# Attention and expert layer on one core: weight decoding in another order, the last bias steps inside the first attention steps

## The chip, the cores and the metric

The kernel runs on one core of one Trainium2 chip. The metric is the device time of one execution in microseconds (us). A core has five engines that run beside each other, each through its own list of instructions in order: TensorE (PE; its weight loads are PEld), VectorE (DVE), ScalarE (ACT), GpSimd (POOL) and SyncE (SP), which here only issues DMA transfers.

## The reference, cut to what matters

```python
B, H, S, D = 4, 8, 576, 64                      # q, k, v: [B, H, S, D]
rel = pos[:, None] - pos[None, :]
x = (log1p(abs(rel)) / log1p(maximum(pos[:, None], 1)))[..., None]
bias = maximum(x @ w1 + b1, 0) @ w2             # 32 hidden units, H outputs
scores = q @ k.T / sqrt(D) + bias.transpose(2, 0, 1)[None]
attn = exp(scores - max(scores)); attn = attn / (sum(attn) + 1e-9)
x = (attn @ v), heads side by side              # [2304, 512]
h = x @ moe_w_in                                # 512 -> 2048
g = s * maximum(h, 0) ** 2 + b
out = g @ moe_w_out                             # 2048 -> 512
```

The two weight matrices arrive as 64-bit numbers and are turned into 32-bit ones on the chip.

## The kernel before, in words

Everything is one function, `attention_moe`, in which the order of the instructions is written out by hand (line 578): each engine gets its instructions in the order in which the code calls them, and the tile library adds the waits. The program has three stages.

**Bias stage** (lines 599 to 604): 36 bias steps of 16 rows each, `STEPS`. `bias_features(st)` makes four feature tiles; `kind` (line 119) says which engine makes each: v is DVE, p is POOL, a is ACT. `bias_step(st)` (line 131) multiplies them by the second weights on PE into one PSUM tile `bps`, from which ACT makes the tile `stg` (line 147), and SP stores `stg` to memory (line 153). For steps 24 to 35 `first_head` also copies the rows of head 0 straight to the tiles `bt` and `be` that the first attention steps add. `bps` lies in the pool `ps_x` (one buffer) in each third step and otherwise in `ps_s` (two buffers). The table `plan` (line 586) says what else is issued behind which bias step: loads, the splits of q and k for pair 0, and the first two scores.

**Attention** (`step`, line 525): 16 pairs of (head, two batches), five steps each, n = 5p + u. Step n turns the probabilities of n (`probs_t`: PE `tps`, copies `pt` by ACT and DVE), computes the scores of n + 2 (PE `sps`, in `ps_s`), adds the bias and takes the maximum on DVE (`biased`, L250), exponentiates on ACT (`expo`, L261) and multiplies the probabilities of pair p - 1 with v (`av`, L366 and L369, in `ps_x`). L369 belongs to u = 4 and so marks each pair once. `split_qk` lets POOL split q (at u = 0) and k (at u = 1) of pair p + 1 into a high and a low part, two instructions each (L211, L212). `norm` (u = 3, L273) makes the reciprocal sums on DVE. `fill()` takes one piece of early weight decoding into a step: eight blocks, each ACT `Abs` (L407), POOL clamp (L409), three DVE bit operations (L411, L414, L417), the high part `wh` on DVE (L426) and the low part `wl` on POOL (L429), six fills a block, at u = 0 to 3 from pair 1 on. A fill stands near the end of its step, and the split of q or k behind it.

**Expert layer** (from line 639): expand (L476) and project (L501) by slots; it also decodes the other 24 weight blocks.

SP issues all loads and stores in one order. Tiles that are placed in memory freed by the bias stage wait for its last users.

```python
        kind = (ends.get(st) or ("vvpa", "vppa", "vpvp")[st % 3])[c]
...
        if st % 3 == 2:
            ps = ps_x.tile([128, 2, 512], F32, tag="x", name="bps")
...
        if st < STEPS - 4 or st == STEPS - 1:
            for i, t in late:
...
        if cur and u < 2:
            split_qk(p + 1, u)
```

Of the kernel before, what the change touches and what calls it, by code (L numbers as in the profile page):

```python
# [9 lines left out]
F32 = mybir.dt.float32  # L10
# [4 lines left out]
ALU = mybir.AluOpType  # L15
# [11 lines left out]
def attention_moe(ctx, tc, q, k, v, w_in, w_out, dist, par, out):  # L27
    nc = tc.nc
    NB, H, S, D = 2 * q.shape[0], q.shape[1], k.shape[3] - 64, q.shape[2] // 2
    DM, DFF = w_out.shape[1], w_out.shape[0]  # L30
    NT = out.shape[0]
# [23 lines left out]
    ps_t = ps_ctx.enter_context(tc.tile_pool(name="ps_t", bufs=2, space=PSUM))  # L55
    pss_ctx = ExitStack()
    ps_s = pss_ctx.enter_context(tc.tile_pool(name="ps_s", bufs=2, space=PSUM, side="right"))
    dctx = ExitStack()
    dp = dctx.enter_context(tc.tile_pool(name="dp", bufs=1, side="right"))
    fp = dctx.enter_context(tc.tile_pool(name="fp", bufs=16, side="right"))  # L60
# [48 lines left out]
        nc.vector.tensor_copy(sb, pt_[:, 2:4])  # L109

    feats, late = {}, []
    ends = {STEPS - 4: "vvvp", STEPS - 3: "vvva", STEPS - 2: "vpva", STEPS - 1: "vpva"}

    def feature(st, c):
        w = NU - S - 16 * st - 4 * c
        f = fp.tile([128, S // 64, 68], F32, tag="f", name="f")[:, :, 0:64]
        src = ls[:, w:w + S].rearrange("p (a b) -> p a b", b=64)
        col = slice(4 * st + c, 4 * st + c + 1)
        kind = (ends.get(st) or ("vvpa", "vppa", "vpvp")[st % 3])[c]
        if kind == "v":  # L120
            nc.vector.tensor_scalar(f, src, thr[:, col], None, op0=ALU.max)
        elif kind == "p":
            nc.gpsimd.tensor_scalar(f, src, FLT_MAX, thr[:, col], op0=ALU.min, op1=ALU.max)
        else:
            nc.scalar.activation(f, src, AF.Relu, bias=off[:, col])
        return f, kind == "a"
# [4 lines left out]
    def bias_step(st):  # L131
        f2, f0, f3, f1 = feats.pop(st)
        fs = (f0, f1, f2, f3)
        if st % 3 == 2:
            ps = ps_x.tile([128, 2, 512], F32, tag="x", name="bps")
        else:
            ps = ps_s.tile([128, 2, 512], F32, tag="s", name="bps")
        pb = ps.rearrange("p a b -> p (a b)")
        for c in range(4):
            nc.tensor.matmul(  # L140
                pb[32 * c:32 * c + 32, 0:512], w2bd, fs[c][0][:, 0:8], start=True, stop=True)
        for c in range(4):
            nc.tensor.matmul(
                pb[32 * c:32 * c + 32, 512:S], w2bd, fs[c][0][:, 8:9], start=True, stop=True)
        kcol = kc[:, 1:2] if fs[3][1] else kc[:, 0:1]
        stg = fp.tile([128, S], F32, tag="stg", name="stg", bufs=10)
        nc.scalar.activation(stg, pb[:, 0:S], AF.Identity, scale=nr[:, st:st + 1], bias=kcol)  # L147
        if st >= 24:
            first_head(st, stg)
        late.append((st, stg))  # L150
        if st < STEPS - 4 or st == STEPS - 1:
            for i, t in late:
                nc.sync.dma_start(out=bias_d[:, 16 * i:16 * i + 16, :].rearrange("h r j -> r h j"), in_=t)
            late.clear()
# [16 lines left out]


    qs, ks, vals, tts, bts, pts, units, accs = {}, {}, {}, {}, {}, {}, {}, {}
    sums, rows, rts, rbs, bes, xts = {}, {}, {}, {}, {}, {}

    def load_bias(p, t0, t1):
        h = pairs[p][0]
# [44 lines left out]
    def scores(n):  # L222
        p, t = divmod(n, 5)
        qt, kt = qs[p], ks[p]
        c = slice(128 * t, 128 * t + 128)
        xs = range(width(n))
        ps = [ps_s.tile([128, 2, 512], F32, tag="s", name="sps") for _ in xs]
        mms = []
        for hf in range(2):
            for x in xs:  # L230
                d = slice(64 * x, 64 * x + 64) if t < 4 else slice(0, 128)
                o = hf * HALF + (64 if x == 0 else 0)
                for i, (a, b) in enumerate(((0, 0), (0, 1), (1, 0))):
                    mms.append((i, hf, x, ps[x][:, hf, 0:HALF], qt[d, a, c], kt[d, b, o:o + HALF]))
        for i, _, _, o, a, b in sorted(mms, key=lambda e: e[1::-1]):
            nc.tensor.matmul(o, a, b, start=(i == 0), stop=(i == 2))  # L236
        units[n] = (
            tp.tile([128, 2, S], F32, tag="pr", name="pr"),
            sm.tile([128, 2], F32, tag="mn", name="mn"),
            ps,  # L240
        )
        if t == 0:
            sums[p] = sm.tile([128, 9], F32, tag="su", name="su")

    def biased(n, x):
        p, t = divmod(n, 5)
# [10 lines left out]
    def expo(n, x):  # L257
        p, t = divmod(n, 5)
        pr, mn, _ = units[n]
        col = 4 * x + t if t < 4 else 8  # L260
        nc.scalar.activation(  # L261
            pr[:, x], tts.pop((n, x)), AF.Exp, bias=mn[:, x:x + 1], scale=-1.0,
            accum_out=sums[p][:, col:col + 1])

    def width(n):
        return 2 if n % 5 < 4 else 1
# [2 lines left out]


    def norm(p):
        su = sums.pop(p)
        nc.vector.tensor_scalar(su, su, 1e-9, None, op0=ALU.add)  # L273
        nc.vector.reciprocal(su, su)
        rows[p] = su

# [12 lines left out]
    def probs_t(n):  # L289
        p, t = divmod(n, 5)  # L290
        if p not in pts:
            pts[p] = (ptp.tile([128, 4, 2, S], F32, tag="pt", name="pt"),
                      ptp.tile([128, S], F32, tag="ptr", name="ptr"))
        pt, ptr = pts[p]
        halves = [slice(64 * r, 64 * r + 64) for r in range(2)]

# [122 lines left out]
        w_full[kind, g, i] = full  # L419
        yield  # L420

    def split_w(kind, g, i):
        full = w_full.pop((kind, g, i))
        hi, lo = w_hi[kind, g][:, i], w_lo[kind, g][:, i]
        if g == 0:
            nc.vector.tensor_copy(hi, full)  # L426
        else:
            nc.scalar.activation(hi, full, AF.Copy)  # L428
        nc.gpsimd.tensor_tensor(lo, full, hi.bitcast(F32), op=ALU.subtract)  # L429


    chunks = [(t0, min(512, NT - t0)) for t0 in range(0, NT, 512)]
    NC = len(chunks)
# [91 lines left out]
    def step(n):  # L525
        p, u = divmod(n, 5)
        m = n + 2
        cur = 0 <= n < LAST
        if cur:
            probs_t(n)  # L530
        if cur and u == 3:
            norm(p)
        if ok(m, 0):
            scores(m)
            for x in range(width(m)):
                biased(m, x)
            expo(m, 0)
        if p >= 1:
            av(p - 1, u, 0)
            av(p - 1, u, 1)  # L540
            if u < 4:
                fill()
        if n == 0:
            load_be(1)
        if u == 4 and cur:
            norm_store(p)
        if u == 0 and p > 0:
            if n <= LAST:
                norm_load(p - 1)
            if p > 1:  # L550
                store_xt(p - 2)
            if cur:
                load_be(p + 1)
                load_v(p + 1)
                load_q(p + 2)
                load_k(p + 2)
        if cur and u < 2:
            split_qk(p + 1, u)
        if cur:
            for e in loads_at.get((p, u), ()):  # L560
                load_bias(*e)

    early = [(kind, 0, i) for kind in range(2) for i in range(4)]

    def early_work():
        for j, e in enumerate(early):
            if j + 2 < len(early):
                load_w(*early[j + 2])
            yield from decode_w(*e)
            split_w(*e)  # L570
            yield

    filler = early_work()

    def fill():
# [12 lines left out]
        11: ((load_bias, 0, 0, 1),),  # L588
        17: ((load_bias, 0, 1, 2),),
        20: ((load_v, 0), (load_be, 0)),  # L590
        28: ((split_qk, 0, 0),),
        30: ((split_qk, 0, 1),),
        26: ((load_bias, 0, 2, 3),),
        33: ((scores, 0), (biased, 0, 0), (expo, 0, 0), (biased, 0, 1)),
        35: ((expo, 0, 1), (scores, 1), (biased, 1, 0),
             (expo, 1, 0), (biased, 1, 1), (load_w, *early[0]), (load_w, *early[1]),
             (load_q, 2), (load_k, 2), (load_v, 1)),
    }
    for st in range(STEPS):
        if st + 2 < STEPS:  # L600
            bias_features(st + 2)
        bias_step(st)
        for fn, *args in plan.get(st, ()):
            fn(*args)
    dctx.close()
    ctx.enter_context(tc.tile_pool(name="pad2", bufs=1, side="right")).tile([128, 40], F32, name="pad2")
    wg0 = ctx.enter_context(tc.tile_pool(name="wg0", bufs=1, side="right", reuse_waits="tile"))
    alloc_w(0, wg0)
    wf = ctx.enter_context(tc.tile_pool(name="wf", bufs=1, side="right", reuse_waits="tile"))
    pctx = ExitStack()  # L610
    ptp = pctx.enter_context(tc.tile_pool(name="ptp", bufs=2, side="right", reuse_waits="tile"))
    decoding = {}

    def late_start(e):
# [5 lines left out]
        for _ in decoding.pop(e):  # L620
            pass

    for n in range(LAST - 2):
        step(n)
        if n == LAST - 10:
            for _ in filler:
                pass
            for a in range(KB - 1):
                load_x(0, a)
        if n == LAST - 4:  # L630
            load_x(0, KB - 1)
# [15 lines left out]
    pctx.close()  # L647
    ps_ctx.close()
    op = ctx.enter_context(tc.tile_pool(name="op", bufs=1, reuse_waits="tile"))
    acc = [op.tile([128, DM], F32, name=f"acc{k}") for k in range(NT // 128)]  # L650
    ps_o = ctx.enter_context(tc.tile_pool(name="ps_o", bufs=1, space=PSUM, reuse_waits="tile"))

    for a in range(KB):
# [104 lines left out]
```

## Time and profile before

| | us |
|---|---|
| median of 3 runs | 686.18 (686.15 to 689.35) |
| the profiled execution | 689.37 |
| its span, first to last instruction | 687.5 |
| PE busy | 665.2 (97%) |
| DVE busy | 456.4 (66%) |
| ACT busy | 353.6 (51%) |
| POOL busy | 181.5 (26%) |
| bias stage, up to the last `bps` | 55 |
| attention, up to the first L476 | 55 to 286 |
| expert layer | 286 to 687 |

The page divides the span among the engines; the trace then gives each instruction's start, its length and, in brackets, how long its engine had been idle and what released it. A share of the whole span says little here, since the three stages have different limits: the last stage is read from the windows, the first two from the timelines of single engines. The profiled execution is the longer kind of the runs: it lies 3.2 us above the median.

### The profile page before, as it was taken

How to read it: one execution, taken by the hardware profiler on the slowest of the kernel's cores; microseconds unless marked ns; L12 is line 12 of the kernel's file. 1: busy time of each engine (PE TensorE's matmuls, PEld its weight loads, DVE VectorE, ACT ScalarE, POOL GpSimd, SP SyncE). 2: the span in 40 equal slices, each digit the busy share in tenths (PEclk: the TensorE clock that was granted, in tenths of full speed). 3: DMA queues.
4: the chain of work that ended last, by engine and by line, in shares of the span. 5: the costliest groups of instructions: out<-in, count | busy, mean ns of one | idle time of the engine just before them, and what ended most of it. 6: DMA issues, size and time to landing. Idle time of an engine off the chain costs nothing.

```text
span 687.5 us, 13641 instructions
## 1 busy us (share of the span) xinstructions
PE 665.2 (97%) x5202; PEld 508.2 (74%) x5202; DVE 456.4 (66%) x883; ACT 353.6 (51%) x741; POOL 181.5 (26%) x190
## 2 busy tenths in 40 slices
PE   8987999999999999999999999999999999999997
PEld 4435667667676667578888888888888888888886
DVE  7996889988898888556576346665446655343344
ACT  6997767777677777534544333332333332322221
POOL 7992362345523450002222012121012220000000
PEclk9999999999999999999999999999999999999999
DMA  5976865656646734378745643216345204333312
GB/s 162 300 233 173 301 206 174 210 190 188 201 147 200 228 114 145 98 235 295 245 153 177 251 153 137 103 37 245 122 154 189 87 35 150 127 119 122 123 61 92
DMA packets 53872, 114.84 MB, mean 167 GB/s; under 512 B 10800, under 2 KB 18224, under 8 KB 53808
## 3 DMA queue, kind: packets, MB, share of 16 engines
q1 hardware_dynamic: 53664, 113.65, 49.8%
q8 instruction: 41, 0.67, 0.4%
q10 hardware_dynamic: 144, 0.33, 0.1%
q14 instruction: 23, 0.19, 0.1%
HBM read 83.77 MB, written 29.56 MB: 165 GB/s over the span
## 4 chain that ended last, share of the span: by engine, by line
PE 85%; DVE 4%; DMA 3%; POOL 3%; ACT 2%; issue 1%; SPq 1%; DVEq 0%; ACTq 0%; POOLq 0%
PE hps L476 29%; PE o L501 28%; PE sps L236 8%; PE xps L366 8%; PE tps L299 5%; PE bps L140 3%; PE xps L369 2%; DMA bias<-stg 2%; DVE tt L250 1%; POOL kr L212 1%; DMA qt<-in_q_dram 1%; POOL wl L429 1%; ACT stg L147 1%; POOL kr L211 1%; DMA pt__123<-in_par_dram 1%
## 5 line engine op out<-in xcount | busy, mean ns | idle before, releaser
L501 PE MATMUL o<-wh,gt 128*128 128x512 f32 x576 | 190.2, 389 | 0.0
L476 PE MATMUL hps<-x,wh 128*128 128x512 f32 (+1 forms) x640 | 181.8, 368 | 0.0
L480 ACT ACTIVATE r<-hps 128x512 f32<-128x512 f32 (+1 forms) x80 | 44.5, 556 | 212.8 <-PE hps L476 212.8
L481 DVE SCALAR_TENSOR_TENSOR r<-r,sb 128x512 f32<-128x512 f32 (+1 forms) x80 | 55.9, 698 | 143.9 <-ACT r L480 143.8
L261 ACT ACTIVATE pr<-tt,mn 128x576 f32<-128x576 f32 x144 | 110.9, 771 | 58.8 <-DVE mn L250 58.4
L476 PEld LDWEIGHTS hps<-x,wh 128*128 128x128 f32 x640 | 116.9, 188 | 22.1 <-ACT x L456 0.4
L501 PEld LDWEIGHTS o<-wh,gt 128*128 128x128 f32 x576 | 108.2, 188 | 22.3
L476 PE MATMUL hps<-x,wl 128*128 128x512 f32 (+1 forms) x320 | 117.7, 368 | 0.0
L501 PE MATMUL o<-wl,gt 128*128 128x512 f32 x288 | 112.2, 390 | 0.0
L429 POOL TENSOR_TENSOR wl<-full,wh 128x512 fp32r<-128x512 f32 x32 | 43.9, 1371 | 213.4 <-ACT wh L428 137.7
L250 DVE CUSTOM_DVE_ANT_0 tt<-sps,bt 128x576 f32<-128x576 f32 x128 | 91.3, 750 | 13.2 <-PE sps L236 12.9
L236 PE MATMUL sps<-kr,qr 64*128 64x288 f32 (+1 forms) x864 | 90.4, 310 | 7.7 <-POOL kr L212 5.1
L486 DVE SCALAR_TENSOR_TENSOR gt<-r,sb,gt 128x512 fp32r<-128x512 f32 (+1 forms) x80 | 62.7, 783 | 38.3 <-ACT gt L485 38.3
L236 PEld LDWEIGHTS sps<-kr,qr 64*128 64x128 f32 (+1 forms) x864 | 70.3, 186 | 12.3 <-POOL kr L212 6.1
L366 PE MATMUL xps<-pt,vt 128*64 128x288 f32 x512 | 77.0, 423 | 1.4 <-DVE rb L374 0.9
L485 ACT ACTIVATE gt<-r,sb 128x512 fp32r<-128x512 f32 (+1 forms) x80 | 54.4, 680 | 45.6 <-DVE r L481 45.5
L299 PEld LDWEIGHTS tps<-ident,pr 64*128 64x128 f32 x1216 | 44.7, 138 | 38.0 <-issue 27.5
L476 PEld LDWEIGHTS hps<-x,wl 128*128 128x128 f32 x320 | 60.3, 188 | 9.9
L501 PEld LDWEIGHTS o<-wl,gt 128*128 128x128 f32 x288 | 54.1, 188 | 10.5
L299 PE MATMUL tps<-ident,pr 64*128 64x64 f32 x1216 | 56.9, 230 | 4.0 <-ACT pt L330 2.0
L409 POOL TENSOR_SCALAR full<-full 128x512 f32<-128x512 f32 x32 | 23.9, 746 | 130.5 <-ACT full L407 130.1
L332 DVE COPY pt<-tps 128x512 f32<-128x512 f32 x64 | 44.0, 687 | 13.1 <-PE tps L299 13.0
(66 smaller groups left out, 704.8 us busy)
## 6 DMA issues: line engine op xcount, KB each, us to landing
x<-xs SPq DMA_DIRECT2D x48, 512.0 KB
bias<-stg SPq DMA_DIRECT2D x36, 288.0 KB
raw<-in_moe_w_in_dram SPq DMA_DIRECT2D x16, 512.0 KB
raw<-in_moe_w_out_dram SPq DMA_DIRECT2D x16, 512.0 KB
xs<-x SPq DMA_DIRECT2D x16, 512.0 KB
bt<-bias SPq DMA_DIRECT2D x7, 1152.0 KB
qt<-in_q_dram SPq DMA_DIRECT2D x16, 320.0 KB
kt<-in_k_dram SPq DMA_DIRECT2D x16, 320.0 KB
```

What stands on the lines that cost most here:

```text
L236: nc.tensor.matmul(o, a, b, start=(i == 0), stop=(i == 2))
L250: nc.vector.tensor_tensor_reduce(tt.rearrange("p (a b) -> p a b", a=2), ps[x][:, :, 0:HALF], bias.rearrange("p (a b) -> p a b", a=2), -1.0 ...
L261: nc.scalar.activation(pr[:, x], tts.pop((n, x)), AF.Exp, bias=mn[:, x:x + 1], scale=-1.0, accum_out=sums[p][:, col:col + 1])
L299: nc.tensor.matmul(outs[r], src[d], ident[d, d], is_transpose=True, start=start, stop=True, skip_group_check=not start)
L366: nc.tensor.matmul(ps[64 * x:64 * x + 64, hf, 0:HALF], vt[:, 4 * x + kb, :], pt[:, kb, x, c], start=(kb == 0), stop=False)
L429: nc.gpsimd.tensor_tensor(lo, full, hi.bitcast(F32), op=ALU.subtract)
L476: nc.tensor.matmul(ps[:, 0:n], w[0, g][:, a, fc], xs_t[s, a][:, j, 0:n], start=(i == 0), stop=(i == 3 * KB - 1))
L480: nc.scalar.activation(r, ps[:, 0:n], AF.Relu)
L481: nc.vector.scalar_tensor_tensor(r, r, sb[:, 0:1], r, op0=ALU.mult, op1=ALU.mult)
L485: nc.scalar.activation(hi, r, AF.Identity, bias=sb[:, 1:2])
L486: nc.vector.scalar_tensor_tensor(lo, r, sb[:, 1:2], hi.bitcast(F32), op0=ALU.add, op1=ALU.subtract)
L501: nc.tensor.matmul(o, gt[:, a, tok], w[1, g][:, fo], start=(fo == 0 and j == 0), stop=(fo == 3 and j == 2))
```

## The change

Four things change.

1. **The end of the bias stage.** The features of steps 32 to 35 are made as v, p, a, p, and are issued behind steps 30 to 33. Steps 30 to 35 all take `ps_x`. The first scores are issued behind step 30, the second behind step 31, attention step 0 behind step 32 and step 1 behind step 35. The stores of `stg` 30 to 35 are issued together after step 35. The q and k splits of pair 0 move from behind steps 28 and 30 to behind 23 and 25, and the loads of q and k for pair 2 and of v for pair 1 from behind step 35 to behind step 28. The buffer `pt` of even pairs gets a place of its own (`ptp0`), later used for part of the output sums.
2. **The splits of q and k** stand right behind `probs_t` in their step, ahead of that step's scores and fill.
3. **Early decoding** takes four fills a block and three fills a pair: the next block's `Abs` and clamp share fills with the present block's bit operations, and the low part `wl` is issued one fill later than `wh`, with the next block's first bit operation.
4. **`norm`** reads the sums from a tile of three rows of four, of which three are used, and writes another tile.

```diff
-    ends = {STEPS - 4: "vvvp", STEPS - 3: "vvva", STEPS - 2: "vpva", STEPS - 1: "vpva"}
...
-        kind = (ends.get(st) or ("vvpa", "vppa", "vpvp")[st % 3])[c]
+        kind = ("vpap" if st >= STEPS - 4 else ("vvpa", "vppa", "vpvp")[st % 3])[c]
...
-        if st % 3 == 2:
+        if st % 3 == 2 or st >= STEPS - 6:
             ps = ps_x.tile([128, 2, 512], F32, tag="x", name="bps")
...
-        if st < STEPS - 4 or st == STEPS - 1:
+        if st < STEPS - 6 or st == STEPS - 1:
             for i, t in late:
...
-            sums[p] = sm.tile([128, 9], F32, tag="su", name="su")
+            sums[p] = sm.tile([128, 3, 4], F32, tag="su", name="su")
...
-        su = sums.pop(p)
-        nc.vector.tensor_scalar(su, su, 1e-9, None, op0=ALU.add)
+        su = sm.tile([128, 9], F32, tag="rw", name="ru", bufs=2)
+        nc.vector.tensor_scalar(
+            su.rearrange("p (a b) -> p a b", a=3), sums.pop(p)[:, :, 0:3], 1e-9, None, op0=ALU.add)
         nc.vector.reciprocal(su, su)
...
             probs_t(n)
+            if u < 2:
+                split_qk(p + 1, u)
         if cur and u == 3:
...
-            if u < 4:
+            if u < 3:
                 fill()
...
-        if cur and u < 2:
-            split_qk(p + 1, u)
...
     def early_work():
+        ahead = {}
+
+        def begin(j):
+            if j < len(early):
+                ahead[j] = decode_w(*early[j])
+                next(ahead[j])
+
+        begin(0)
+        yield
+        next(ahead[0])
+        yield
         for j, e in enumerate(early):
             if j + 2 < len(early):
                 load_w(*early[j + 2])
-            yield from decode_w(*e)
-            split_w(*e)
+            next(ahead[j])
+            if j > 0:
+                split_lo(*early[j - 1])
             yield
+            next(ahead[j])
+            begin(j + 1)
+            yield
+            next(ahead[j])
+            if j + 1 < len(early):
+                next(ahead[j + 1])
+            yield
+            split_hi(*e)
+            yield
+        split_lo(*early[-1])
...
-        28: ((split_qk, 0, 0),),
-        30: ((split_qk, 0, 1),),
+        23: ((split_qk, 0, 0),),
+        25: ((split_qk, 0, 1),),
         26: ((load_bias, 0, 2, 3),),
-        33: ((scores, 0), (biased, 0, 0), (expo, 0, 0), (biased, 0, 1)),
-        35: ((expo, 0, 1), (scores, 1), (biased, 1, 0),
-             (expo, 1, 0), (biased, 1, 1), (load_w, *early[0]), (load_w, *early[1]),
-             (load_q, 2), (load_k, 2), (load_v, 1)),
+        28: ((load_q, 2), (load_k, 2), (load_v, 1)),
+        30: ((scores, 0), (biased, 0, 0), (biased, 0, 1), (expo, 0, 0), (bias_features, 32)),
+        31: ((expo, 0, 1), (scores, 1), (biased, 1, 0), (biased, 1, 1), (expo, 1, 0),
+             (bias_features, 33)),
+        32: ((step, 0), (bias_features, 34)),
+        33: ((bias_features, 35),),
+        35: ((step, 1), (load_w, *early[0]), (load_w, *early[1])),
     }
     for st in range(STEPS):
-        if st + 2 < STEPS:
+        if st + 2 < STEPS - 4:
             bias_features(st + 2)
         bias_step(st)
...
-    for n in range(LAST - 2):
+    for n in range(2, LAST - 2):
```

`split_lo` and `split_hi` are the two halves of the old `split_w`: the POOL subtraction and the copy of the high part.

**ACT at the end of the bias stage, from `stg` 31 before.** Before:

```order
L147 ACTIVATE stg<-bps,kc,pt__123 128x576
L125 ACTIVATE f<-ls,off 128x9x64
L147 ACTIVATE stg<-bps,kc,pt__123 128x576
L261 ACTIVATE pr,su<-tt,mn 128x576
L147 ACTIVATE stg<-bps,kc,pt__123 128x576 x2
L261 ACTIVATE pr,su<-tt,mn 128x576 x3
L330 ACTIVATE pt<-tps 128x8x64
```

Now, from `stg` 29 and 30:

```order
L147 ACTIVATE stg<-bps,kc,pt__130 128x576 x2
L261 ACTIVATE pr,su<-tt,mn 128x576
L125 ACTIVATE f<-ls,off 128x9x64
L147 ACTIVATE stg<-bps,kc,pt__130 128x576
L261 ACTIVATE pr,su<-tt,mn 128x576 x2
L125 ACTIVATE f<-ls,off 128x9x64
L147 ACTIVATE stg<-bps,kc,pt__130 128x576
L261 ACTIVATE pr,su<-tt,mn 128x576
L332 ACTIVATE pt<-tps 128x8x64
L261 ACTIVATE pr,su<-tt,mn 128x576
L125 ACTIVATE f<-ls,off 128x9x64
L147 ACTIVATE stg<-bps,kc,pt__130 128x576
```

Before, all `stg` but two were made ahead of the first exponential (L261); now five come behind it, each between exponentials, features and the copy `pt`. Behind these rows follow one feature, `stg` 34 and 35, and only then the rest of step 1.

**PE at the same place, from the first scores on.** Before:

```order
L236 MATMUL sps<-kr,qr 128x288 x12
L140 MATMUL bps<-f,pt__123 32x512 x4
L143 MATMUL bps<-f,pt__123 32x64 x4
L140 MATMUL bps<-f,pt__123 32x512 x4
L143 MATMUL bps<-f,pt__123 32x64 x4
L236 MATMUL sps<-kr,qr 128x288 x12
L299 MATMUL tps<-ident,pr 128x64 x16
L236 MATMUL sps<-kr,qr 128x288 x12
L299 MATMUL tps<-ident,pr 128x64 x16
```

Now:

```order
L236 MATMUL sps<-kr,qr 128x288 x12
L140 MATMUL bps<-f,pt__130 32x512 x4
L143 MATMUL bps<-f,pt__130 32x64 x4
L236 MATMUL sps<-kr,qr 128x288 x12
L140 MATMUL bps<-f,pt__130 32x512 x4
L143 MATMUL bps<-f,pt__130 32x64 x4
L301 MATMUL tps<-ident,pr 128x64 x16
L236 MATMUL sps<-kr,qr 128x288 x12
L140 MATMUL bps<-f,pt__130 32x512 x4
L143 MATMUL bps<-f,pt__130 32x64 x4
L140 MATMUL bps<-f,pt__130 32x512 x4
L143 MATMUL bps<-f,pt__130 32x64 x4
```

One more pair of rows (`bps` 35) and the second `tps` follow. Between the first and the second `tps` (steps 0 and 1) stand three bias steps now, and none before.

**POOL from its first instructions of the bias stage on.** Before:

```order
L123 TENSOR_SCALAR f<-ls,thr 128x9x64 x51
L211 TENSOR_SCALAR qr<-qt 128x640
L212 TENSOR_TENSOR qr<-qt,qr 128x640
L123 TENSOR_SCALAR f<-ls,thr 128x9x64 x3
L211 TENSOR_SCALAR kr<-kt 128x640
L212 TENSOR_TENSOR kr<-kt,kr 128x640
L123 TENSOR_SCALAR f<-ls,thr 128x9x64 x2
```

Now:

```order
L123 TENSOR_SCALAR f<-ls,thr 128x9x64 x43
L211 TENSOR_SCALAR qr<-qt 128x640
L212 TENSOR_TENSOR qr<-qt,qr 128x640
L123 TENSOR_SCALAR f<-ls,thr 128x9x64 x3
L211 TENSOR_SCALAR kr<-kt 128x640
L212 TENSOR_TENSOR kr<-kt,kr 128x640
L123 TENSOR_SCALAR f<-ls,thr 128x9x64 x11
```

Both splits of pair 0 stand eight features earlier, and four more features follow behind the q split of pair 1.

## Rows read from the trace of the kernel before

**Rows 1.** Windows: stretch, length, each engine's busy us, granted PE clock, DMA share, GB/s.

```profile
290.00:687.00 397.00, 393.80 (x1830) 328.26 (x1826) 210.87 (x312) 135.54 (x232) 52.48 (x48) 1.00 0.42 149
```

**Rows 2.** Timeline of PE, the u = 4 mark of pairs 0, 1, 12, 13.

```profile
83.43 1.24 PE L369 MATMUL xps<-ptr,vt 128*128 128x288 f32 x4
100.75 1.24 PE L369 MATMUL xps<-ptr,vt 128*128 128x288 f32 x4
...
256.68 1.24 PE L369 MATMUL xps<-ptr,vt 128*128 128x288 f32 x4
270.14 1.24 PE L369 MATMUL xps<-ptr,vt 128*128 128x288 f32 x4
```

**Rows 3.** Timelines of POOL and PE around step 13; in brackets idle time and releaser.

```profile
92.17 1.28 POOL L429 TENSOR_TENSOR wl<-full,wh 128x512 fp32r<-128x512 f32 x1 [2.92 <-DVE wh L426]
94.22 1.54 POOL L212 TENSOR_TENSOR kr<-kt,kr 128x640 fp32r<-128x640 f32 x1
...
95.82 1.15 PE L236 MATMUL sps<-kr,qr 64*128 64x288 f32 x10 [1.23 <-POOL kr L212]
```

**Rows 4.** Window right behind that wait, columns as in the first group.

```profile
96.00:100.00 4.00, 4.00 (x35) 2.37 (x36) 1.49 (x5) 1.63 (x4) 3.75 (x5) 0.57 1.01 355
```

**Rows 5.** Waits of PE (total us, times, longest), and its wait in pair 1.

```profile
PE sps L236 <- POOL kr L212: 5.1, 5, 1.2
...
79.99 0.92 PE L236 MATMUL sps<-kr,qr 64*128 64x288 f32 x10 [1.11 <-POOL kr L212]
```

**Rows 6.** DVE by line, 60 to 300 us: min/median/max ns, first and last start.

```profile
L414 DVE SCALAR_TENSOR_TENSOR full<-raw,full x8: 685/686/1993, 82.3 to 236.7; 128x512 uint32<-128x512 uint32 x8
L273 DVE TENSOR_SCALAR su<-su x16: 161/165/1260, 66.1 to 280.9; 128x9 f32<-128x9 f32 x16
```

**Rows 7.** Timelines of POOL and DVE in the bias stage; the q split lies between.

```profile
5.51 36.81 POOL L123 TENSOR_SCALAR f<-ls,thr 128x576 f32<-128x576 f32 x51 [4.21 <-DVE ls L100]
...
44.88 2.18 POOL L123 TENSOR_SCALAR f<-ls,thr 128x576 f32<-128x576 f32 x3
...
35.73 15.91 DVE L121 TENSOR_SCALAR f<-ls,thr 128x576 f32<-128x576 f32 x22
```

**Rows 8.** Timeline of PE: first scores, bias step 34, second `tps`.

```profile
51.35 1.05 PE L236 MATMUL sps<-kr,qr 64*128 64x288 f32 x11 [1.03 <-ACT stg L147]
53.14 1.06 PE L140 MATMUL bps<-f,pt__123 128*32 128x512 f32 x8 [0.74 <-DVE mn L250]
54.02 0.29 PE L143 MATMUL bps<-f,pt__123 128*32 128x64 f32 x8
...
59.28 0.71 PE L299 MATMUL tps<-ident,pr 64*128 64x64 f32 x16 [0.40 <-ACT pt L330]
```

**Rows 9.** Timelines of DVE and ACT: bias added, `stg`, feature, exponential, copy, first block.

```profile
52.32 0.76 DVE L250 CUSTOM_DVE_ANT_0 tt<-sps,bt 128x576 f32<-128x576 f32 x1 [0.68 <-PE sps L236]
...
49.09 0.82 ACT L147 ACTIVATE stg<-bps,kc,pt__123 128x576 f32<-128x576 f32 x1
49.81 0.77 ACT L125 ACTIVATE f<-ls,off 128x576 f32<-128x576 f32 x1
...
57.89 0.76 ACT L261 ACTIVATE pr<-tt,mn 128x576 f32<-128x576 f32 x1
...
58.65 0.57 ACT L330 ACTIVATE pt<-tps 128x512 f32<-128x512 f32 x1
...
72.99 0.65 ACT L407 ACTIVATE full<-raw 128x512 f32<-128x512 f32 x1
```

**Rows 10.** SP's issues, DVE's first `be`, and a window of the transfers behind them.

```profile
57.62 4.98 SPq L165 DMA_DIRECT2D be<-stg  x8
62.64 2.53 SPq L153 DMA_DIRECT2D bias<-stg  x4
...
64.38 0.76 DVE L250 CUSTOM_DVE_ANT_0 tt<-sps,be 128x576 f32<-128x576 f32 x1 [0.88 <-ACT pt L330]
...
64.00:74.00 10.00, 8.42 (x121) 6.40 (x121) 8.31 (x23) 8.19 (x22) 0.00 (x0) 1.00 0.96 302
```

More of the change, by code (lines that the diff above doesn't have):

```diff
@@ L57, in attention_moe @@
     ps_s = pss_ctx.enter_context(tc.tile_pool(name="ps_s", bufs=2, space=PSUM, side="right"))
+    ctx.enter_context(tc.tile_pool(name="pad2", bufs=1, side="right")).tile([128, 40], F32, name="pad2")
+    ptp0 = ctx.enter_context(tc.tile_pool(name="ptp0", bufs=1, side="right"))
     dctx = ExitStack()
@@ L173, in attention_moe @@
     qs, ks, vals, tts, bts, pts, units, accs = {}, {}, {}, {}, {}, {}, {}, {}
-    sums, rows, rts, rbs, bes, xts = {}, {}, {}, {}, {}, {}
+    sums, rows, rts, rbs, bes, xts, ptps = {}, {}, {}, {}, {}, {}, [ptp0]
     def load_bias(p, t0, t1):
@@ L262, in expo @@
             pr[:, x], tts.pop((n, x)), AF.Exp, bias=mn[:, x:x + 1], scale=-1.0,
-            accum_out=sums[p][:, col:col + 1])
+            accum_out=sums[p][:, col // 3, col % 3:col % 3 + 1])
     def width(n):
@@ L291, in probs_t @@
         if p not in pts:
-            pts[p] = (ptp.tile([128, 4, 2, S], F32, tag="pt", name="pt"),
-                      ptp.tile([128, S], F32, tag="ptr", name="ptr"))
+            pool = ptps[p % 2]
+            pts[p] = (pool.tile([128, 4, 2, S], F32, tag="pt", name="pt"),
+                      pool.tile([128, S], F32, tag="ptr", name="ptr"))
         pt, ptr = pts[p]
@@ L420, in decode_w, with split_hi @@
         yield
-    def split_w(kind, g, i):
-        full = w_full.pop((kind, g, i))
-        hi, lo = w_hi[kind, g][:, i], w_lo[kind, g][:, i]
+    def split_hi(kind, g, i):
+        full = w_full[kind, g, i]
+        hi = w_hi[kind, g][:, i]
         if g == 0:
@@ L428, in split_w, with split_lo @@
             nc.scalar.activation(hi, full, AF.Copy)
+    def split_lo(kind, g, i):
+        full = w_full.pop((kind, g, i))
+        hi, lo = w_hi[kind, g][:, i], w_lo[kind, g][:, i]
         nc.gpsimd.tensor_tensor(lo, full, hi.bitcast(F32), op=ALU.subtract)
+    def split_w(kind, g, i):
+        split_hi(kind, g, i)
+        split_lo(kind, g, i)
     chunks = [(t0, min(512, NT - t0)) for t0 in range(0, NT, 512)]
@@ L605, in attention_moe @@
     dctx.close()
-    ctx.enter_context(tc.tile_pool(name="pad2", bufs=1, side="right")).tile([128, 40], F32, name="pad2")
     wg0 = ctx.enter_context(tc.tile_pool(name="wg0", bufs=1, side="right", reuse_waits="tile"))
@@ L610, in attention_moe @@
     pctx = ExitStack()
-    ptp = pctx.enter_context(tc.tile_pool(name="ptp", bufs=2, side="right", reuse_waits="tile"))
+    ptps.append(pctx.enter_context(tc.tile_pool(name="ptp1", bufs=1, side="right", reuse_waits="tile")))
     decoding = {}
@@ L649, in attention_moe @@
     op = ctx.enter_context(tc.tile_pool(name="op", bufs=1, reuse_waits="tile"))
-    acc = [op.tile([128, DM], F32, name=f"acc{k}") for k in range(NT // 128)]
+    first = ptp0.tile([128, 9, DM], F32, tag="pt", name="acc")
+    acc = [first[:, k] for k in range(9)]
+    acc += [op.tile([128, DM], F32, name=f"acc{k}") for k in range(9, NT // 128)]
     ps_o = ctx.enter_context(tc.tile_pool(name="ps_o", bufs=1, space=PSUM, reuse_waits="tile"))
```

## The prediction

> **What bounds the kernel now.** I read the windows first, to see which stages can change at all. From 290 us to the end PE is busy for 393.8 of 397 us at the full clock, 2.4 GHz [rows 1]. The change touches nothing there, so only the moment at which that stage begins can move, and the end moves with it one for one.
>
> Next the timeline of PE with one mark per pair (u = 4). Between pairs 12 and 13 it takes 13.46 us; there PE waits for nothing and sets the pace. From pair 0 to pair 13 it is 186.71 us, where 13 undisturbed intervals would take 174.98 [rows 2]. So 11.7 us are lost in attention behind pair 0, the first 3.86 of them between the marks of pairs 0 and 1 (17.32 instead of 13.46).
>
> Then the waits, to see why. PE waits 5.1 us in five places for POOL's split of k [rows 5]. Around step 13 one sees how: POOL stands at the low part `wl` until DVE has made `wh`, the split of k is queued behind it, and PE gets its scores 1.23 us late [rows 3]. Right after this wait the granted clock is 0.57 over four microseconds, so PE spent most of them at 1.2 GHz [rows 4]; that costs about 4 x 0.43 = 1.7 us. A third kind of loss is on DVE: one bit operation of the decoding, normally 0.69 us, once takes 1.99, and `norm`, normally 0.16, once takes 1.26 [rows 6].
>
> Last the timelines at the end of the bias stage, which show what the other half of the change leans on. POOL makes 51 features without a gap, 0.722 us each, and DVE 22 in 15.91 us, also 0.72 each [rows 7]. POOL has no slack there.
>
> **Part 1, splits and decoding: a gain.** The split moves ahead of the fill in its step. In the new order POOL meets `wl` one fill after `wh` was issued to DVE, and the clamp one fill after its `Abs`; neither is then late. The scores that need the split of k come two steps after it, some 5 us. So the waits for POOL should go: 1.1 us in pair 1 [rows 5], and all or nearly all of the 11.7 us behind pair 0's mark, since clock loss and weight-load waits hang on the same places. What is late next is nothing but PE itself. The bit operations still read two tensors beside POOL's splits, and the new order only shifts when they meet; I keep 0.4 us for a chance meeting and book -1.1 - 11.3 = -12.4. Bounds: if only the 4.0 us of POOL waits behind pair 0 and the clock's 1.7 go, -6.8; at best -12.8. I take the upper end, because the intervals that are free of decoding trouble now are clean to 0.1 us. The fills per block fall from six to four at three a pair, so decoding still ends near pair 12; its number of instructions is the same.
>
> **Part 2, the end of the bias stage: a loss.** Worked along one chain.
>
> - POOL reaches the last feature of step 29 after 50 features and both splits of pair 0. A split takes 44.88 - 42.32 = 2.56 us [rows 7], so 5.51 + 50 x 0.722 + 2 x 2.56 = 46.7 us. Before, the 50th feature was ready at 41.6, since both splits stood behind it.
> - Steps 29 to 35 now share the one buffer `ps_x`: matmuls, then ACT's `stg`, then the next matmuls. A step's matmuls take 54.31 - 53.14 = 1.17 us until the last ends [rows 8], `stg` 0.82 [rows 9]. Step 29 is through at 46.7 + 1.17 + 0.82 = 48.7, step 30's matmuls (1.06) end at 49.8, and the first scores start there, 1.5 us ahead of 51.35 before [rows 8].
> - DVE started 0.97 us after the scores (51.35 to 52.32) and takes 0.76, so ACT begins the first exponential at 51.5. From there to the end of `stg` 33 it has twelve instructions in its list: five exponentials, three features, three `stg`, one copy. Back to back they take 0.76, 0.72, 0.72 (49.09 to 49.81) and some 0.5 us [rows 9], together 3.8 + 4.3 + 0.5 = 8.6, so 60.1. Their inputs come from DVE and PE earlier than ACT needs them, as far as I can follow them.
> - Step 34's matmuls had to wait for this `stg`: 60.1 + 1.17 + 0.82 = 62.1, and step 35's 1.06 us end at 63.2. Only then comes the second `tps`, at 59.28 before [rows 8]: **+3.9 us**.
>
> Behind this the steps of pair 0 run as before. The tile `be` is no new limit: its transfers from `stg` 35 (ready at 64.1) are issued by 65.4 and land 1.8 us later (62.60 to 64.38), while DVE used `be` 5.1 us after the second `tps` [rows 8, 10], now 68.3.
>
> **Part 3, the first weight block: a loss.** Its load stood ahead of the tile `bt` of pair 2 and behind four stores; now it is behind six stores and behind `bt`. ACT wanted it at 72.99, or 13.71 us after the second `tps` [rows 8, 9], so now at 76.9. SP issues the six stores (0.63 us each) from 65.4 on. By the tiles' shapes 6 x 288 + 1152 + 128 + 512 KB, or 3.6 MB, go first; at 302 GB/s [rows 10] that is 11.9 us from the first landing issue at 66.0, so 77.9, and up to 1.8 more until it lands. I take 79.0, a stall of ACT of 2.1 us, which holds the next copy and PE with it: **+2.0 us**. Bounds: 0, if the loads run faster than the stores that make most of that window, and 3, if all runs as slowly as the stores. The loads of q, k and v that moved forward now stand ahead of the last copies to `bt` on SP, three issues which I take at the 0.63 us of a store; PE's later first use of those rows leaves room for them.
>
> `norm` issues the same instructions as before. `ptp0` takes memory, not time.
>
> **The sum.** -12.4 + 3.9 + 2.0 = -6.5 us against the profiled execution, 689.37, gives **682.9 us**. The median is 3.2 us below that execution, so against it the gain is only 3.3 us, 0.48%: the shorter runs evidently lack some of the losses that I take away, by size the late k of step 13 with its lower clock. A measurement of this kernel can tell about 0.5% from no change, which is 3.4 us. The forecast lies just inside.
>
> **The rivals.**
>
> *The block lands in time* (0.15). The loads of `bt` and of the block run faster than the window of mostly stores; then Part 3 costs nothing: 680.9. For it: the window is an average, and the last transfers in it are loads. Against: 3.6 MB would have to pass between 66.0 and some 75.1 us, at nearly 400 GB/s.
>
> *`norm` is still held up* (0.14). Each hold costs 1.26 - 0.16 = 1.1 us [rows 6], and POOL's split of q, which now comes first in the step, may start near u = 3, where `norm` stands. In four pairs of 15 that is 4.4 us: 687.3, no change. Against: DVE's features, written with gaps as the new sums are read, ran at 0.72 us beside a POOL that never paused [rows 7]. [...]
>
> *TensorE falls to 1.2 GHz in the new first steps: slower* (0.11). The waits between bias steps there are longer than any at present: `stg` 32 is seventh of ACT's twelve and ends at 56.7, step 33's matmuls at 57.9, and step 34 starts at 60.1, 2.2 us later. The trace shows the fall after a wait of 1.23 us [rows 4]. At half speed the matmuls on my chain double: steps 29, 30, 34 and 35 (4.5 us), the first scores (1.0), and the stretch behind the wait for the weight block loses another 1.7: +7.2, 690.1. It is slower than the median's bound of 689.6 only if nearly all of this stretch runs so, from 6.7 us on. Against: after the waits of 1.03 and 0.74 us ahead of the first scores and step 34 the matmuls took 1.05 and 1.06 us [rows 8], the same, so that stage did not lose its clock. [...]
>
> *The order does not free POOL* (0.06). If the k splits are late because the transfer of k is, not because of `wl`, Part 1 gives nothing and Parts 2 and 3 remain: 695.3. Against: the rows of step 13 show the split running directly behind `wl` [rows 3].
>
> **The numbers.** The forecast has 0.54, with a range of its own of 681.3 to 685.5 (Part 3's bounds, a clock loss of 1.7 us). Of it 0.22 falls below 682.75, the bound of faster. Faster: 0.22 + 0.15 = 0.37. Within 0.5%: 0.32 + 0.14 = 0.46. Slower: 0.11 + 0.06 = 0.17. The range is 680.3 to 690.0: from the block in time to a full clock loss; the last rival and the tails stay out.
>
> **What would show it.** Right: the second `tps` near 63.2 us, ACT idle about 2 us on the first raw block, the u = 4 mark of pair 0 near 88 and then every 13.46 us, no wait of PE for POOL's k. Wrong, step by step: a second `tps` before 61 or after 65 (Part 2), an ACT that does not wait for the block (Part 3), marks that are still 15 us apart in some pairs or bit operations of 2 us (Part 1), a granted clock below 1 between 50 and 82 us (third rival).

## The result, and the profile after

| | before | after |
|---|---|---|
| median, us | 686.16 (6 runs) | 693.74 (6 runs, 691.9 to 695.27) |
| the profiled execution | 689.37 | 692.12 |
| its span | 687.5 | 690.3 |
| u = 4 mark of pair 0 | 83.43 | 91.92 |
| from there to the mark of pair 13 | 186.71 | 175.60 |
| first `hps` of the expert layer | 285.59 | 282.99 |
| from there to the end of the span | 401.9 | 407.3 |

The changed kernel is slower: the ratio of its times to those before is 1.0094, with a 95% interval of 1.0072 to 1.0116. The forecast was 682.9 us, faster or even; the range ended at 690.0. The experiments below were timed in three sets, each beside its own runs of the kernel before (medians of 686.25 to 686.89 us), and their ratios, with 95% intervals in brackets, are to these. One of the ten runs of experiment 7 took 917.64 us at a granted clock of 0.654; the ratio leaves it out.

In the two profiled executions the stretches of the table add up: +8.5 us up to the mark of pair 0, -11.1 from there to pair 13, nothing between there and the first `hps`, and +5.4 in the expert layer, together the +2.8 us of the span. The forecast had +4.8, -11.3 and 0.

First the timeline of PE with one mark per pair, which answers to [rows 2]:

```profile
91.92 1.24 PE L371 MATMUL xps<-ptr,vt 128*128 128x288 f32 x4
105.38 0.99 PE L371 MATMUL xps<-ptr,vt 128*128 128x288 f32 x3
...
254.07 1.24 PE L371 MATMUL xps<-ptr,vt 128*128 128x288 f32 x4
267.52 0.75 PE L371 MATMUL xps<-ptr,vt 128*128 128x288 f32 x2
```

Both intervals shown are the undisturbed 13.46 us of before, and so are all thirteen to 0.2 us. The three largest waits of PE between 40 and 290 us (total, times, longest) show where new ones stand:

```profile
PE bps L140 <- ACT stg L147: 5.0, 5, 2.2
PE bps L140 <- POOL f L123: 3.3, 2, 2.6
PE tps L301 <- ACT pt L332: 2.3, 2, 1.7
```

The wait for POOL's k, 5.1 us before [rows 5], is gone from the full list too. `norm` and the bit operation of [rows 6] are never long up to the end of attention: `norm` takes 152 to 154 ns in all 16 places.

Second the end of the bias stage, timeline of PE (answers to [rows 8]), and below it windows (columns as in [rows 1]; the eighth figure, behind POOL's, is the granted clock):

```profile
45.16 0.63 PE L140 MATMUL bps<-f,pt__130 128*32 128x512 f32 x3 [2.57 <-POOL f L123]
...
49.75 1.06 PE L140 MATMUL bps<-f,pt__130 128*32 128x512 f32 x8 [1.02 <-ACT stg L147]
50.63 0.29 PE L143 MATMUL bps<-f,pt__130 128*32 128x64 f32 x8
50.86 1.05 PE L236 MATMUL sps<-kr,qr 64*128 64x288 f32 x12
...
61.34 1.06 PE L140 MATMUL bps<-f,pt__130 128*32 128x512 f32 x8 [2.20 <-ACT stg L147]
62.23 0.29 PE L143 MATMUL bps<-f,pt__130 128*32 128x64 f32 x8
63.52 1.93 PE L140 MATMUL bps<-f,pt__130 128*32 128x512 f32 x8 [1.00 <-ACT stg L147]
65.23 0.44 PE L143 MATMUL bps<-f,pt__130 128*32 128x64 f32 x8
65.60 1.04 PE L301 MATMUL tps<-ident,pr 64*128 64x64 f32 x16
```

```profile
46.00:48.00 2.00, 2.00 (x18) 0.59 (x14) 0.00 (x0) 1.30 (x2) 2.00 (x4) 0.50 0.65 173
...
64.00:66.00 2.00, 2.00 (x24) 0.79 (x18) 0.00 (x0) 0.22 (x1) 0.00 (x0) 0.50 0.12 37
...
78.00:80.00 2.00, 2.00 (x9) 0.77 (x8) 1.44 (x4) 0.87 (x2) 0.00 (x0) 0.50 1.09 365
```

The second `tps` comes at 65.60, 6.3 us later than before and 2.4 later than forecast. Twice in this stretch PE runs at half the full clock (0.50 granted from 46 to 48 and from 64 to 66 us), behind waits of 2.57 and of 2.20 and 1.00 us; `bps` 35 then takes 1.93 us instead of 1.06. A third stretch at that clock follows (0.50 from 78 to 80 us); between the second `tps` and it PE waits for no longer than 0.52 us at a time. At the full clock, 1.00, twelve matmuls of 512 columns take 2.72 us in the kernel before and twelve of 256 take 1.43, so 3072 columns more take 1.29 us, some 2.4 a ns: that answers to the forecast's 2.4 GHz, and a granted 0.50 to its 1.2.

Third the first weight block, timelines of ACT and PE:

```profile
82.98 0.66 ACT L409 ACTIVATE full<-raw 128x512 f32<-128x512 f32 x1 [3.17 <-DMA raw<-in_moe_w_in_dram]
...
84.94 0.71 PE L301 MATMUL tps<-ident,pr 64*128 64x64 f32 x15 [1.73 <-ACT pt L332]
```

ACT waits 3.17 us for the block (2.1 forecast), and PE 1.73 us for the copy queued behind.

Last the expert layer, where the profile by waits shows nothing: from 290 to 690 us PE is busy for 396.6 of 400 us at a granted clock of 1.00. This is the timeline of PE, from which only the first row of each group is copied: a group is the 12 matmuls of one expand (`hps`) or project (`o`).

```profile
323.82 0.40 PE L510 MATMUL o<-wh,gt 128*128 128x512 f32 x1
326.62 0.63 PE L485 MATMUL hps<-x,wh 128*128 128x512 f32 x2
329.38 0.40 PE L510 MATMUL o<-wh,gt 128*128 128x512 f32 x1
...
426.53 0.61 PE L485 MATMUL hps<-x,wh 128*128 128x512 f32 x2
429.25 0.39 PE L510 MATMUL o<-wh,gt 128*128 128x512 f32 x1
431.97 0.61 PE L485 MATMUL hps<-x,wh 128*128 128x512 f32 x2
```

The `o` group at 323.82 takes 2.80 us and the `hps` group behind it 2.76; at 426 both take 2.72, as nearly every group of 512 columns did before:

```profile
342.04 0.39 PE L501 MATMUL o<-wh,gt 128*128 128x512 f32 x1
...
344.76 0.62 PE L476 MATMUL hps<-x,wh 128*128 128x512 f32 x2
...
347.48 0.39 PE L501 MATMUL o<-wh,gt 128*128 128x512 f32 x1
```

So PE works some 3% more slowly in part of the layer, with the same matmuls. The view of matmuls by line shows it as a mean of 392 against 389 ns (between 300 and 680 us; before, then after):

```profile
L501 PE MATMUL o<-wh,gt 128*128 128x512 f32 x563 | 186.1, 389 | 0.0
```

```profile
L510 PE MATMUL o<-wh,gt 128*128 128x512 f32 x553 | 184.3, 392 | 0.0
```

What differs is where the tiles lie, by the addresses that the two programs give them (a trace has none). `norm`'s new tile `ru` has two buffers of 36 bytes that take 64 each, so everything allocated behind it on that side of the memory moves by 128 bytes: `gt`, the pool `xp` (x of odd slots) and `wa` (weights of groups 1 and 3) went from 64 to 192 past a multiple of 256. `wraw` (x of even slots) lies ahead of it and `wg0` (weights of groups 0 and 2) on the other side; both stayed at 64. The slow groups are those whose two operands, the stationary and the moving one, lie at different places modulo 256. The kernel's unused tiles `pad0` to `pad2` set these places.

### The profile page after: what moved, and what is told of

Read it like the earlier page. It is cut to its first block, busy times and chain, and to the rows that moved or that the text cites. A ratio compares the mean times of both kernels' runs of the same rounds, so it can differ in the third digit from the quotient of the medians.

```text
span 690.3 us, 13640 instructions
## 1 busy us (share of the span) xinstructions
PE 669.2 (97%) x5202; PEld 507.4 (74%) x5202; DVE 444.9 (64%) x877; ACT 353.9 (51%) x742; POOL 184.7 (27%) x195
## 3 DMA queue, kind: packets, MB, share of 16 engines
q1 hardware_dynamic: 53664, 113.65, 49.6%
## 4 chain that ended last, share of the span: by engine, by line
PE 86%; ACT 2%; DMA 1%; SPq 1%; DVE 1%; issue 0%; DVEq 0%; ACTq 0%
PE hps L485 29%; PE o L510 29%; PE xps L368 10%; PE sps L236 9%; PE tps L301 6%; PE xps L371 3%; DMA raw<-in_moe_w_in_dram 1%; SPq L153 1%; ACT pr L261 0%; PE xps L301 0%; ACT stg L147 0%; DVE tt L250 0%; PE bps L140 0%; ACT full L409 0%; DVE acc L516 0%
## 5 line engine op out<-in xcount | busy, mean ns | idle before, releaser
L261 ACT ACTIVATE pr<-tt,mn 128x576 f32<-128x576 f32 x144 | 110.8, 770 | 46.1 <-DVE mn L250 45.7
L236 PE MATMUL sps<-kr,qr 64*128 64x288 f32 (+1 forms) x864 | 86.9, 308 | 0.6 <-DVE mn L250 0.4
```

The source lines that it names most:

```text
L261: nc.scalar.activation(pr[:, x], tts.pop((n, x)), AF.Exp, bias=mn[:, x:x + 1], scale=-1.0, accum_out=sums[p][:, col // 3, col % 3:col % 3 ...
```

## The experiments

**1 to 3: the places of the tiles.** Three kernels change one number each, the length of an unused tile:

```diff
-    ...tile_pool(name="pad1", bufs=1)).tile([128, 32], F32, name="pad1")
+    ...tile_pool(name="pad1", bufs=1)).tile([128, 64], F32, name="pad1")
```

in the changed kernel and in the kernel before, and `pad2` from 40 to 72 in the changed kernel.

> The changed kernel with the unused tile pad1 128 bytes longer, so that gt, xp, wa and all else behind it lie again at the places modulo 256 at which they lay before (64 past a multiple of 256, like the weights in wg0 and x in wraw). Theory A (matmuls are slower when the stationary and the moving tile differ by 128 bytes modulo 256): all groups of 12 matmuls of the expert layer back to 2.72 us, that layer from 407.2 to 401.8 us, the kernel from 693.7 to 688.3. Theory B (the layer is slower because the weights of wg0 and nine of the sums lie in another region, where ptp0 puts them): no change, 693.7, groups of 2.80 stay. Theory C (the clock, or records of this one execution): no change in the median either.

> The kernel before with pad1 128 bytes longer, nothing else: gt, xp and wa move to 192 modulo 256, wg0 and wraw stay at 64. Theory A: the expert layer takes 407.2 instead of 401.8 us with the pattern of the changed kernel (project 2.80 in the weight groups held in wg0 and 2.72 in those in wa; expand 2.80 or 2.72 by the pool of x), the kernel 686.2 + 5.4 = 691.6. Theories B and C: 686.2, all groups 2.72.

> The changed kernel with the other unused tile, pad2, 128 bytes longer: wg0 goes to 192 modulo 256 as well, only x in wraw stays at 64. Theory A, with the difference between the two tiles as the cause: all project groups 2.72; expand slow (2.79) where x is in wraw (even slots), in all four weight groups, and 2.72 in odd slots; 36 full groups x 0.07 = 2.5 us lost against an aligned kernel, so 688.3 + 2.5 = 690.8. Theory A', with the place itself as the cause (tiles at 192 are slow whatever the other is): project slow in all four weight groups, the kernel above 693.7. Theory B: 693.7.

Measured: 688.63, 693.19 and 690.94 us beside 686.89 before (ratios 1.0026 [1.0000, 1.0051], 1.0093 [1.0059, 1.0127], 1.0068 [1.0044, 1.0093]). Theory A holds three times: the changed kernel gets its 5 us back, the kernel before loses 6 by a pad alone, and the third lies where counting its slow groups put it (the trace has 32 full ones, 4 fewer than I counted, which is 0.3 us). The matmuls by line of the first and the second:

```profile
L510 PE MATMUL o<-wh,gt 128*128 128x512 f32 x562 | 185.8, 389 | 0.0
```

```profile
L501 PE MATMUL o<-wh,gt 128*128 128x512 f32 x552 | 183.9, 392 | 0.0
```

The group starts of the third tell the difference from the place itself, in an even slot and then in an odd one:

```profile
326.67 0.62 PE L485 MATMUL hps<-x,wh 128*128 128x512 f32 x2
329.46 0.39 PE L510 MATMUL o<-wh,gt 128*128 128x512 f32 x1
332.19 0.62 PE L485 MATMUL hps<-x,wh 128*128 128x512 f32 x2
...
348.77 0.61 PE L485 MATMUL hps<-x,wh 128*128 128x512 f32 x2
351.49 0.39 PE L510 MATMUL o<-wh,gt 128*128 128x512 f32 x1
```

With weights and `gt` both at 192, `o` takes 2.73 us, where it took 2.80; `hps` takes 2.79 with x at 64 and 2.72 with x at 192.

**4 and 5: the two halves alone.** The order alone has the diff's hunks on `step`, `early_work` and `split_w`; its complement has all others but `norm`'s. Neither has the tile `ru`.

> The kernel before with only the new places of the splits and the new order of the early decoding; bias stage and norm as before (so no tile ru, and no tile moves). If that half gives what its trace shows in the changed kernel (11.1 us between the marks of pairs 0 and 13, and the 1.1 us wait of pair 1), the profiled time is near 676, between 674.5 and 678, as the median of before has some 3 us less to lose. The rival, that most of the 11 us came from pair 0 and 1 starting later and with more work done ahead: no more than 5 us, 681 or above.

> The changed kernel without its new order of splits and decoding and without the new norm (no ru, so tiles lie aligned): the new end of the bias stage alone, with pair 0's splits behind steps 23 and 25, the early attention steps, the moved loads and ptp0. Theory: it loses what the two halves together lack, that is the realigned changed kernel 688.6 less the order alone 682.6, 6.0 us: 686.9 + 6.0 = 692.9, with the second tps near 66 us and the mark of pair 0 near 92 to 94. Rival: the loss comes only where both halves meet (POOL and ACT in steps 1 to 5); then 687 to 689.

Measured: 682.61 us (0.9937 [0.9908, 0.9967]) and 696.06 (1.0135 [1.0109, 1.0162]). The order gains 4.3 us. That lies outside the 674.5 to 678 I expected and where the rival had put it, but not for the rival's reason: experiment 8 keeps the old end of the bias stage and has 175.85 us between the marks of pairs 0 and 13, as short as after the change. What the order alone lacks is `norm`. The new end loses 9.2, 3.2 more than expected, since I had taken the whole gain of the other half from the order alone. In the order alone PE never waits for POOL's k, but some intervals between marks are still long, 14.80 us in one pair. Its DVE and POOL there:

```profile
148.09 1.50 DVE L273 TENSOR_SCALAR su<-su 128x9 f32<-128x9 f32 x1
```

```profile
148.01 1.55 POOL L212 TENSOR_TENSOR qr<-qt,qr 128x640 fp32r<-128x640 f32 x1
149.52 1.27 POOL L433 TENSOR_TENSOR wl<-full,wh 128x512 fp32r<-128x512 f32 x1
```

`norm` stands until POOL's split ends at 149.56, the maxima behind it are late, and PE waits for them at 150.5. Six of the 16 `norm` are held in this run, for 0.29 to 1.50 us, each until an instruction of POOL's split ends; the others take 0.16 to 0.17.

**8: the order with the new `norm`**, aligned by the pad of the first experiment.

> The order alone (e4_order_alone) with the new norm too (sums in three rows of four, tile ru) and pad1 128 bytes longer so that nothing else loses its place. If the held norm costs PE time, part of the 16 x (340 - 153) ns = 3.0 us of DVE comes back, and intervals of 14 to 14.8 us between marks become 13.5: 682.6 - 2 = 680.6. If norm lies beside PE's work: 682.6.

Measured: 679.67 us (0.9891 [0.9866, 0.9915]), the fastest of all. `norm` by line (min/median/max ns):

```profile
L273 DVE TENSOR_SCALAR ru<-su x16: 152/154/164, 66.8 to 270.5; 128x9 f32<-128x9 f32 x16
```

It is never held, though six of the 16 start while a split of POOL's is running (at 149.02 us 1.46 before its end), and all intervals between marks are 13.45 to 13.67 us up to pair 13. Of the 2.9 us against the order alone I take the direction as shown, since place and mechanism show in the trace; the two ratios' intervals still overlap at their ends.

Order and `norm` (-7.2), the end of the bias stage (+9.2) and the shift (+5.1 to +6.3) add up to 7.1 to 8.3 us; the change cost 7.6.

**6, 7 and 9: what makes the new end slow.** In the realigned changed kernel the first two blocks are loaded at bias step 28, or pair 0's splits stand there, or both:

```diff
-        23: ((split_qk, 0, 0),),
-        25: ((split_qk, 0, 1),),
-        28: ((load_q, 2), (load_k, 2), (load_v, 1)),
+        28: ((split_qk, 0, 0), (split_qk, 0, 1), (load_q, 2), (load_k, 2), (load_v, 1),
+             (load_w, *early[0]), (load_w, *early[1])),
...
-        35: ((step, 1), (load_w, *early[0]), (load_w, *early[1])),
+        35: ((step, 1),),
```

> The realigned changed kernel with the loads of the first two weight blocks issued behind bias step 28 instead of 35. Theory (the late block holds ACT for 3.2 us, and TensorE runs at the low clock behind that hold): ACT no longer waits for the block, the wait of PE for ACT's pt at 85 us goes, pair 0's mark 2.5 to 4 us earlier, the kernel 688.6 - 3 = 685.6. Rival: the megabyte of loads now delays the rows of bias that pairs 0 and 1 need, and the time stays at 688.6 or rises.

> The realigned changed kernel with both splits of pair 0 behind bias step 28 on POOL, instead of 23 and 25. If the two splits ahead of the features are what delays the end of the bias stage, the wait of 2.57 us for POOL before step 28 goes, the clock does not fall there, and the first scores wait for k at 5.51 + 54 x 0.722 + 2 x 2.56 = 49.6 us instead of starting at 50.9: second tps 1.3 us earlier, the kernel near 687.3. If the single buffer ps_x and ACT's list set the end whatever POOL does, second tps stays at 66 and the kernel at 688.6.

> The realigned changed kernel with both edits: pair 0's splits behind step 28 and the first two weight blocks loaded behind step 28. If the two losses are separate, 688.6 - 3.9 - 3.3 = 681.4; a little less, 680.5, since the later-splits kernel alone waited 3.4 us for ACT's pt behind its weight block and then ran at the low clock. Then the new end of the bias stage is even with the old one (order and norm with the old end: 679.7), not better. Rival: one loss hides the other, 685.

Measured: 684.80 us (0.9964 [0.9947, 0.9980]), 685.28 (0.9966 [0.9950, 0.9983]) and 681.33 (0.9931 [0.9905, 0.9957]). Beside 688.6 that is -3.8, -3.3 and -7.3 (by the ratios 0.6, 0.6 and 0.95%): within the noise two separate losses that add up, and the rival's 685 lies outside the interval of 9. With both mended the new end is no better than the old one: 1.7 us above experiment 8, with intervals that overlap at their ends. The first `Abs` with the blocks loaded early:

```profile
81.93 0.65 ACT L409 ACTIVATE full<-raw 128x512 f32<-128x512 f32 x1
```

ACT does not wait. With the later splits alone the first scores start at 46.69 us, 4.2 earlier than after the change; I had put them at 49.6, having counted three POOL features too many ahead of them. The splits were thus more of the loss than I expected of this run, though part of it came back at the weight block, for which ACT then waited 3.77 us.

**10: a shorter ACT list.** As 9, with the last bias steps' third feature on DVE ("vpap" becomes "vpvp").

> As e9, and the last four bias steps' third feature made by DVE instead of ACT (v, p, v, p). If ACT's list of twelve is what the last bias steps wait for (the wait of 2.2 us before step 34), three features of 0.72 us leave it and second tps comes some 2 us earlier: 678.5 if e9 gives 680.5. If DVE's own work there (maxima of the first scores) or ps_x sets it: as e9.

Measured: 682.56 us (0.9940 [0.9911, 0.9970]), no better than 9. PE's wait before `bps` 34 in 9, and in 10:

```profile
57.19 1.74 PE L140 MATMUL bps<-f,pt__130 128*32 128x512 f32 x8 [2.20 <-ACT stg L147]
```

```profile
58.01 1.06 PE L140 MATMUL bps<-f,pt__130 128*32 128x512 f32 x8 [2.22 <-DVE f L121]
```

The wait has the same length and another releaser: DVE, which also makes the maxima, takes ACT's place as the last.

The two traces also show how little one execution says of the clock. In 9 steps 34 and 35 take 1.74 and 1.93 us, in 10 both take 1.06, and in 7, behind the same 2.20 us, they take 1.07 and 1.81: like waits are followed by either clock. So in 10 the second `tps` comes 0.9 us earlier than in 9, and the mark of pair 0 still 1.9 later, with a granted clock of 0.50 from 72 to 76 us, where 9 has the full one.

**11 and 12: how much difference is enough.** The kernel before, `pad1` 64 and 32 bytes longer.

> The kernel before with pad1 64 bytes longer: gt, xp and wa at 128 modulo 256, wg0 and wraw at 64. If any difference modulo 256 is slow: groups of 2.79 to 2.80 us as with 128 bytes, some 692. If only a difference of 128 is: all 2.72, 686.9. If it grows with the difference: groups near 2.76, 690.

> The same with 32 bytes: gt, xp and wa at 96 modulo 256. If any difference modulo 256 is slow: some 692 with groups of 2.79 to 2.80 us; if only 128 is: 686.9 with all groups 2.72; if it grows with the difference: groups near 2.74, 688.5.

Measured: 691.22 us (1.0081 [1.0052, 1.0110]) and 694.26 (two runs; 1.0110 [1.0068, 1.0151]). Groups with unlike operands take 2.79 to 2.80 us in both, but for some `hps` groups of the first, at 2.76. The loss does not grow with the difference, and 32 bytes are enough. The matmuls by line of the second:

```profile
L501 PE MATMUL o<-wh,gt 128*128 128x512 f32 x554 | 185.0, 393 | 0.0
```

## Why the prediction was wrong

**The step that failed** is in its first paragraph: "The change touches nothing there, so only the moment at which that stage begins can move." The diff does not touch the expert layer's code, but the tile `ru` moves its operands by 128 bytes, and PE's rate depends on that (2.79 to 2.80 instead of 2.72 us for a group): +5.4 us in the profiled execution, 5 to 6 in the medians (experiments 1 and 2). None of the rivals had it. The sentence "`norm` issues the same instructions as before" stood beside it: I read the new tile as an instruction's output and not as a place in memory. Without this step the kernel would have come out at 688.6, against a median before of 686.9: inside my range, and with a ratio of 1.0026 within the 0.5% that the prediction calls no change, but not at 682.9. The forecast was -3.3 us against the median, and +7.6 came; of these 10.9 the shift is 5.1 to 6.3, the new end of the bias stage 3.3 (+9.2 where Parts 2 and 3 had 5.9), and order and `norm` 2.0 (-7.2 where Part 1 leaves -9.2).

**Part 1 was right in the profiled execution.** From pair 0 to pair 13 it forecast -11.3 us and -11.1 came; no wait for k, no 15 us interval. The experiments divide it: the order removes the waits for POOL's k (-4.3 in the medians), `norm` in its new form stops being held (some -2.9 more). I booked all of it to the order. One reason is that [rows 6] gives the longest case of each kind, which the prediction reads as the only one: in the trace of the kernel before six of the 16 `norm` were held, for 0.40 to 1.26 us, 3.2 us of DVE together. In the medians the two give -7.2, where -12.4 less the 3.2 us by which the profiled execution lay above the median makes -9.2.

**The rival of the held `norm`** did not occur, and experiments 4 and 8 show the difference: nine values read in one row and written in place were held for up to 1.50 us, three rows of three written to one row of nine in another tile never, with 1498 against 164 ns as the longest of 16. Why the one is held and the other not is open: no run tells the shape from the other tile, and the shape alone does not decide: the reciprocal behind it, also nine into nine, takes 215 to 217 ns in experiment 8 even where it starts while a split is running, seven times of 16.

The first rival and the last did not occur either: ACT did wait for the block, and in experiment 4 PE has no wait for POOL's k.

**Part 2 was mis-sized.** The second `tps` came at 65.60, not 63.2. The chain was the right one: ACT's list behind the first scores, then two rounds through `ps_x`. Its twelve entries took from 52.75 to 61.29, 8.5 us where I had 8.6. What the sum left out is the clock, which stood among the rivals. Step 29's matmuls started at 46.59, within 0.1 of the forecast, but ran at half the full clock (0.50 from 46 to 48 us) behind the 2.57 us wait for POOL, so its `stg` ended at 49.7 instead of 48.7; `bps` 35 lost another 0.87 in the same way. These two make 1.9 of the 2.4 us. My slower rival named this loss, but for the whole stretch, at +7.2 us, and behind the wait ahead of step 34 alone; I set it aside because waits of 1.03 and 0.74 us before had left the clock alone [rows 8], and then forecast a longer one myself. Both signs that the prediction had named for this came: a second `tps` after 65 us, and a granted clock below 1 between 50 and 82 (0.50 from 64 to 66 us).

**Part 3 was mis-sized for ACT and near for PE; what the forecast lacked here is again the clock.** ACT waited 3.17 us, not 2.1. The block was ready at 82.98 instead of 79.0; 2.4 of these 4.0 us are Part 2's, since `stg` 35 came late and SP issued the stores ahead of the block from 67.8 on and not from 65.4. ACT's own need of it moved by 2.9, to 79.81. PE lost 1.73 us to this wait, where 2.0 were booked.

The mark of pair 0 came 8.5 us late, not 4.8, and 2.4 of the difference is Part 2's. The rest is the third stretch at half the full clock, from 76.5 us on (0.50 from 78 to 80 us): eleven matmuls of the scores took 1.70 us and eight of `xps` 2.12, against 1.05 and 1.19 at the full clock, 1.6 us together. So 1.73 and 1.6, less the 1.1 us wait for k that is gone, make the 2.2 by which this mark is later than the second `tps` is. Why the clock falls there is open. In the trace of experiment 1, the same program but for a pad, it is full from 70 to 86 us and falls behind the wait for the block instead (0.57 from 86 to 88 us). Loading the blocks earlier is worth 3.8 us in the medians (experiment 6), and the clock of that trace is full from 72 to 90 us.

## What to carry to other kernels

A tile of a few bytes can slow matmuls far away in the program by moving their operands (here two buffers of 36 bytes, 2.79 to 2.80 instead of 2.72 us for a group of twelve): after any change to pools, compare the places of the operands of the longest matmul loop modulo 256, and compare the mean matmul duration before looking at waits. Where work is moved to fill a stage, ask which of its engines has the shorter list there; here the moved bias steps met ACT and POOL, which had no slack (ACT's twelve entries took 8.5 us back to back, POOL's eleven features behind its k split 7.92). And take a change apart: its order of splits and its `norm` alone beat both kernels at 679.67 us, 7.2 below the kernel before.

## What the runs showed of the hardware that I had not expected

Twelve matmuls of 512 columns of 32-bit numbers, back to back at the full clock, take 2.72 us when the stationary and the moving tile start at the same place modulo 256 bytes, and nearly always 2.79 to 2.80 when they differ, whether by 32, 64 or 128; other differences were not tried. (Modulo 512, `gt` and the weights in `wa` lie 256 apart in the kernel before, and their groups take 2.72 us all the same.) It is the relation that counts, not the place: both at 64 and both at 192 are fast (2.72 us before, 2.72 to 2.73 in experiment 3). An `hps` group with like operands between two slow `o` groups takes some 2.76. Groups of 256 columns show no difference (1.43 us before, 1.42 to 1.44 after), and neither do the 288-column matmuls of attention, whose `pt` and `vt` lie alike before and 128 bytes apart after the change (a mean of 419 ns in both from 100 to 270 us). Why this is so, no run here shows.
